# Attention products on four 64x64 TensorE tiles, in bursts inside pass 2

## The chip, the cores and the metric

One core of one Trainium2 chip runs the whole program. The metric is the device time of one execution in microseconds (us), as a median over executions. Engines: TensorE (PE, with PEld for its weight loads), VectorE (DVE), ScalarE (ACT), GpSimd (POOL), and SyncE (SP), which here only starts transfers.

## The reference, cut to what matters

```python
# q, k, v: [8 batches, 8 heads, 576 rows, 64]
q_s = softmax(q, axis=-1)            # over the 64
k_s = softmax(k, axis=2)             # over the 576 rows
kv  = einsum('bhsd,bhse->bhde', k_s, v)      # 64x64 per head
out = einsum('bhsd,bhde->bhse', q_s, kv)
x   = out as [4608 tokens, 512]
h   = x @ w_in                       # [512, 2048]
y   = (h * sigmoid(beta * h)) @ w_out        # [2048, 512], 4608x512 out
```

The two large products are most of the work. Attention is small, but its contraction (64) and its output (64) fill half of the 128*128 weights, which the trace shows for the large products, in each direction.

## The kernel before

The kernel cuts the 4608 tokens into nine slabs of 512: eight hold 512 rows of one batch each, and the ninth holds the 64 remaining rows of all eight. Pass 1 of a slab is 64 products with `w_in` and 16 Silus; pass 2 is 64 products with `w_out`. Products of a later batch's attention are put between them. Two heads share a product: the keys of the pair are laid out block-diagonally with zeros, so that one 128x128 weight holds both.

```python
# keys and values: 9 products for each pair of heads, 36 per batch, 65 columns each
# (the 65th column of v is 1 and gives the softmax denominator)
l, r_, ke, kv, ko = kv_rows(b, hp, j)        # l = EK[i][:, hp, j, 0:128], half zeros
mm(PS[bk][:, VW * n:VW * n + D + 1], l, r_[:, 0:D + 1], j == 0, j == NG - 1, ...)

# output: one product of 512 columns per pair, 4 per batch; KVD is block-diagonal too
mm(PS[bk][:, :], KVD[i][:, hp, :], QT[i][:, hp, :], True, True, ...)

def attn(b):                                 # b = slab + 1; numbers are places in the slab
    s = spread(kv_steps(b, (0, 1, 2, 3)), 8, 36)         # amid pass 1
    ...                                                  # four outputs in 84 to 108
    if b % 2: s += spread(outr_steps(b), 104, 120)       # remaining rows of two batches
```

A small recording layer orders the engines.

```python
def add(self, eng, fn, r=(), w=(), bank=(), ...):
    for k in w:                              # whoever read or wrote what this overwrites
        for d in self.readers.get(k, ()): deps.append(d)
    ...
def plan(self):
    for op in self.ops:
        for d in op.deps:
            d.inc = True                     # d is to raise its engine's semaphore
```

The softmax here doesn't subtract the row's maximum and nothing guards it: scores larger than these inputs give would overflow.

## Time and profile before

| | before |
|---|---|
| time, median | 284.99 us (284.67 to 285.23, 3 runs) |
| profiled span | 283.6 us |
| TensorE busy | 97% |

The page and the stretches of the kernel before are shown and priced in the prediction. A burst, below, is a run of products on tiles with no product of the whole array between them.

### The profile page before, as it was taken

How to read it: one execution, taken by the hardware profiler on the slowest of the kernel's cores; microseconds unless marked ns; L12 is line 12 of the kernel's file. 1: busy time of each engine (PE TensorE's matmuls, PEld its weight loads, DVE VectorE, ACT ScalarE, POOL GpSimd, SP SyncE). 2: the span in 40 equal slices, each digit the busy share in tenths (PEclk: the TensorE clock that was granted, in tenths of full speed). 3: DMA queues.
4: the chain of work that ended last, by engine and by line, in shares of the span. 5: the costliest groups of instructions: out<-in, count | busy, mean ns of one | idle time of the engine just before them, and what ended most of it. 6: DMA issues, size and time to landing. Idle time of an engine off the chain costs nothing.

```text
span 283.6 us, 3916 instructions
## 1 busy us (share of the span) xinstructions
PE 276.3 (97%) x1575; PEld 136.4 (48%) x1606; DVE 116.4 (41%) x217; ACT 177.2 (62%) x242; POOL 39.3 (14%) x58
## 2 busy tenths in 40 slices
PE   7899999999999999999999999999999999999995
PEld 3545454445455445544554445444544445444443
DVE  4655686208791348124741564055705300110012
ACT  5667777989977936796479737892660076017500
POOL 6632041216122032100130000000000000000000
PEclk9799999999999999999999999999999999999999
DMA  7999999999998999207970033002700030012022
GB/s 244 375 391 399 391 369 301 364 345 236 321 345 235 363 354 308 39 21 255 373 112 1 2 148 74 2 1 92 132 19 0 0 150 0 0 49 102 0 74 74
DMA packets 41466, 50.07 MB, mean 177 GB/s; under 512 B 20324, under 2 KB 28772, under 8 KB 40296
## 3 DMA queue, kind: packets, MB, share of 16 engines
q1 hardware_dynamic: 40496, 48.77, 55.4%
q10 hardware_dynamic: 952, 1.06, 1.1%
q8 instruction: 12, 0.20, 0.3%
q14 instruction: 6, 0.05, 0.0%
HBM read 36.71 MB, written 9.44 MB: 163 GB/s over the span
## 4 chain that ended last, share of the span: by engine, by line
PE 93%; DMA 3%; SPq 2%; issue 1%; POOL 1%; DVE 0%; POOLq 0%
PE PS L373 92%; DMA WST<-in_moe_w_in_dram 3%; SPq L259 1%; POOL WIN L580 1%; SPq L249 0%; PE PS L371 0%; SPq L576 0%; DVE O2S L732 0%; POOLq L140 0%
## 5 line engine op out<-in xcount | busy, mean ns | idle before, releaser
L654 ACT ACTIVATE GT<-PS,BETA 128x512 bf16<-128x512 f32 x144 | 96.7, 689 | 79.7 <-PE PS L373 79.6
L373 PE MATMUL PS<-WOUT,GT 128*128 128x512 bf16 (+2 forms) x580 | 131.8, 373 | 0.6
L373 PE MATMUL PS<-XT,WIN 128*128 128x512 bf16 x560 | 130.7, 379 | 0.5
L373 PEld LDWEIGHTS PS<-XT,WIN 128*128 128x128 bf16 x576 | 60.2, 106 | 58.9 <-ACT GT L654 0.4
L373 PEld LDWEIGHTS PS<-WOUT,GT 128*128 128x128 bf16 x592 | 55.4, 98 | 61.8
L711 DVE COPY O2S<-PS 128x512 f32<-128x512 f32 x33 | 22.7, 687 | 107.7 <-PE PS L373 107.7
L373 PE MATMUL PS<-VB,EK 128*128 128x65 bf16 x252 | 33.3, 193 | 0.4
L358 POOL CAST VB<-VF 128x576 bf16<-128x576 f32 x29 | 21.6, 746 | 77.9 <-DMA VF<-in_v_dram 48.8
L309 ACT ACTIVATE EK<-KF 64x1152 bf16<-64x1152 f32 x24 | 27.8, 1158 | 0.4
L339 DVE TENSOR_REDUCE QS<-EQ 128x8 f32<-128x512 bf16 (+1 forms) x22 | 20.1, 913 | 16.0 <-ACT EQ L297 15.8
L373 PEld LDWEIGHTS PS<-VB,EK 128*128 128x128 bf16 x252 | 20.0, 98 | 6.5
L449 DVE CAST XT<-PS 128x512 bf16<-128x512 f32 x24 | 16.4, 690 | 10.9 <-PE PS L373 10.9
L297 ACT ACTIVATE EQ<-QF 128x512 bf16<-128x512 f32 x32 | 17.8, 619 | 1.4 <-DMA QF<-in_q_dram 1.2
L341 DVE TENSOR_TENSOR EQ<-EQ,QI 128x1024 bf16<-128x1024 bf16 (+1 forms) x14 | 15.9, 1133 | 0.5
L373 PE MATMUL PS<-QT,KVD 128*128 128x512 bf16 x29 | 11.2, 387 | 0.2
L341 POOL TENSOR_TENSOR EQ<-EQ,QI 128x512 bf16<-128x512 bf16 x8 | 8.3, 1044 | 18.4 <-DVE QI L340 18.1
L411 DVE TENSOR_TENSOR KVD<-PS,RC 64x64 bf16<-64x64 f32 (+2 forms) x28 | 8.6, 308 | 0.9
L297 ACT ACT_TABLE_LOAD x6 | 7.7, 1283 | 0.1
L373 PE MATMUL PS<-XT 128*128 128x512 f32 x6 | 5.5, 1088 | 1.5 <-DVE XT L219 1.5
L654 ACT ACT_TABLE_LOAD x5 | 6.4, 1283 | 0.1
L373 PEld LDWEIGHTS PS<-QT,KVD 128*128 128x128 bf16 x32 | 3.1, 98 | 5.6 <-DVE KVD L411 1.2
L432 DVE RECIPROCAL RC<-PS 128x4 f32<-128x4 f32 (+2 forms) x9 | 1.6, 176 | 10.0 <-PE PS L373 9.9
(54 smaller groups left out, 90.0 us busy)
## 6 DMA issues: line engine op xcount, KB each, us to landing
out_dram<-O2S SPq DMA_DIRECT2D x8, 1024.0 KB, 5.0
KF<-in_k_dram SPq DMA_DIRECT2D x6, 1152.0 KB, 9.0
VF<-in_v_dram SPq DMA_DIRECT2D x6, 1152.0 KB, 11.3
QF<-in_q_dram SPq DMA_DIRECT2D x6, 1024.0 KB, 7.6
KF<-in_k_dram SPq DMA_DIRECT2D x8, 288.0 KB, 8.6
VF<-in_v_dram SPq DMA_DIRECT2D x8, 288.0 KB, 9.0
WST<-in_moe_w_in_dram SPq DMA_DIRECT2D x8, 256.0 KB, 8.1
O2S<-in_moe_w_in_dram SPq DMA_DIRECT2D x4, 512.0 KB, 11.4
```

The costliest lines, as they stand in the source:

```text
L259: add(engs[c % len(engs)], lambda e, a=a, o=o: e.dma_start(o, a), w=[(name, i, hp) for hp in range(c * n, c * n + n)], slot=f"{name}{i}_{c}")
L297: add(ACTE, lambda e, o=o, a=a: e.activation(o, a, ACT.Exp), r=[("qf", i, hp)], w=[("eq", i, hp)])
L309: add(ACTE, lambda e, o=o, a=a: e.activation(o, a, ACT.Exp), r=[("kf", i, h) for h in hps], w=[("ek", i, h, e_) for h in hps])
L339: add(DVE, lambda e: e.tensor_reduce(s_, a, AX.X, ALU.add), r=ks, w=[("qs", i, hp0)])
L341: add(eng, lambda e: e.tensor_tensor(a, a, vb, ALU.mult), r=ks + [("qi", i, hp0)], w=ks)
L358: add(eng, lambda e: (e.copy if eng == ACTE else e.tensor_copy)(o, a), r=[("vf", i, hp), ("vone", i)], w=[("vb", i, hp, h) for h in ((0, 1 ...
L373: add(PE, lambda e: e.matmul(o, l, r_, start=start, stop=stop, tile_position=tp), r=r, w=w, bank=[bk])
L411: add(DVE, lambda e, o=o, a=a, s_=s_: e.tensor_tensor(o, a, s_, ALU.mult), r=[("ps", bk)] + [("rc", i, h) for h in hps], w=[("kvd", i, h, ...
L449: add(eng, lambda e: (e.copy if eng == ACTE else e.tensor_copy)(XT[i][:, hp, :], PS[bk][:, :]), r=[("ps", bk)], w=[("xt", i, hp)], bank=[bk])
L580: add(eng, lambda e: e.tensor_copy(WIN[:, m, 512 * c:512 * c + 512], STAGE[c][:, m, :]), r=[SKEY[c][m]], w=[("win", c, m)])
L654: add(ACTE, lambda e: e.activation(GT[:, f, :], PS[bk][:, :], ACT.Silu, scale=BETA[:, f:f + 1]), r=[("ps", bk), "beta"], w=[("gt", f)], ba ...
L711: add(eng, lambda e: (e.copy if eng == ACTE else e.tensor_copy)(O2S[t % 2][:, u, :], PS[bk][:, :]), r=[("ps", bk)], w=[("o2", t % 2, u)], ...
```

## The change: its intent and its core

The intent is to stop multiplying zeros. The array is used as four independent 64x64 tiles: four products, a quad of two heads of one pair and two of the next, are to run at once. The kernel puts the tiles of an odd pair off the diagonal, so a head whose keys stand in partitions 0 to 63 has its result written to 64 to 127; therefore the queries of odd pairs are loaded with their two heads swapped. The keys need no zeros any more, so one exponential covers 128 partitions. The tile products stand in bursts, since going between the full array and tiles costs time (0.22 us in the one burst of the kernel before).

```diff
+        def quad(hp):     # (pair, first row, first column of the tile)
+            return ((hp, 0, 0), (hp, 64, 64), (hp + 1, 0, 64), (hp + 1, 64, 0))
+        def kv_quads(b, bks, halves=(0, 2)):
+            for a in halves:
+                for j in range(NG):
+                    for hp, ro, co in quad(a):
+                        tile_mm(bks[hp % 2], ro, co, VW * (a // 2), D + 1,
+                                EK[i][p, hp, j, :], VB[i][p, hp, j, 0:D + 1], ...)
+        def out_quads(b, bks): ...     # 8 products of 512 columns, 2 evictions on ACT, 2 on DVE
+        def outr_quads(b, bks): ...    # 16 products of 64 columns
-        def attn(b):
-            s = spread(kv_steps(b, (0, 1, 2, 3)), 8, 36)
...
-                todo = spread(outr_steps(1), 101.5, 103) + attn_late(2)
+                todo = spread(outr_steps(1), 94, 95)
+                todo += [(95, lambda: kv_a(2)), (103, lambda: kv_b(2)),
+                         (117, lambda: block(2, True)), (125, lambda: kv_b(3))]
+            elif t < 7 and t % 2 == 0:
+                todo = [(80, lambda: block(t + 1, False))]      # 8 outputs + 16 remainders
+                if t + 2 < B:
+                    todo += [(93, lambda: kv_a(t + 2)), (101, lambda: kv_b(t + 2))]   # 36 + 36
             elif t < 7:
-                todo = attn(t + 1)
+                todo = [(93, lambda: block(t + 1, True)), (101, lambda: kv_b(t + 2))] # 44 + 36
...
-            load_main("qf", qt_h, QF, b)
+            load_swapped(b)            # four transfers in place of one
```

More of the change, by code (lines that the diff above doesn't have):

```diff
@@ L181, in bass_efficient_attn_shen__then__act_swish_beta_kernel @@
         EQ = [sb(f"EQ{i}", [128, NHP, 4, 2, D], BF16) for i in range(2)]
-        EK = [sb(f"EK{i}", [128, NHP, NG, 2 * D], BF16) for i in range(2)]
+        EKD = sb("EKD", [128, NHP, NG, 2 * D], BF16)
+        EK = [sb(f"EK{i}", [128, NHP, NG, D], BF16) for i in range(2)]
         EQR = [sb(f"EQR{i}", [128, H, D], BF16) for i in range(2)]
@@ L191, in bass_efficient_attn_shen__then__act_swish_beta_kernel @@
         KVD = [sb(f"KVD{i}", [128, NHP, 128], BF16) for i in range(2)]
+        KVC = [sb(f"KVC{i}", [128, NHP, D], BF16) for i in range(2)]
         RC = [sb(f"RC{i}", [128, NHP], F32) for i in range(2)]
@@ L232, in homes_vk, with homes_ek @@
                 add(POOL, lambda e, z=z: e.memset(z.bitcast(F32), 0.0), w=[("kvz", i, e_)])
-        def homes_ek(i, e_, r=()):
-            z = EK[i][64 * e_:64 * e_ + 64, :, :, 64 * (1 - e_):64 * (2 - e_)]
-            add(POOL, lambda e: e.memset(z.bitcast(F32), 0.0), r=r, w=[("ekz", i, e_)])
+        def homes_ek(e_):
+            z = EKD[64 * e_:64 * e_ + 64, :, :, 64 * (1 - e_):64 * (2 - e_)]
+            add(POOL, lambda e: e.memset(z.bitcast(F32), 0.0), w=[("ekz", e_)])
         def src(th, b, h0, nh):
@@ L262, in load_qrem @@
         def load_qrem(b):
+            i = b // 2 % 2
             for h in range(2):
-                a = bass.AP(qt_h, (b + h) * H * S * D + SM * D, [[D, SR], [S * D, H], [1, D]])
-                i = b // 2 % 2
-                add(SP, lambda e, h=h, a=a: e.dma_start(QRF[i][64 * h:64 * h + 64, :, :], a),
-                    w=[("qrf", i, h)], slot=f"qrf{i}{h}")
+                q0 = (b + h) * H * S * D + SM * D
+                if b == 0:
+                    a = bass.AP(qt_h, q0, [[D, SR], [S * D, H], [1, D]])
+                    add(SP, lambda e, h=h, a=a: e.dma_start(QRF[i][64 * h:64 * h + 64, :, :], a),
+                        w=[("qrf", i, h)], slot=f"qrf{i}{h}")
+                    continue
+                for x, (s0, d0, n) in enumerate(SLOTS):
+                    a = bass.AP(qt_h, q0 + s0 * S * D, [[D, SR], [n * S * D, 2], [1, D]])
+                    o = bass.AP(QRF[i], 64 * h * H * D + d0 * D,
+                                [[H * D, 64], [n * D, 2], [1, D]])
+                    add(SP, lambda e, o=o, a=a: e.dma_start(o, a),
+                        w=[("qrf", i, h, x)], slot=f"qrf{i}{h}{x}")
         def load_k(b, split=1, cs=None, engs=(SP,)):
@@ L273, in load_v, with load_swapped @@
             load_pairs("vf", vt_h, VF, b, split, cs)
+        SLOTS = ((0, 0, 1), (4, 4, 1), (2, 3, 4), (3, 2, 4))
+        def load_swapped(b):
+            i = b % 2
+            for x, (s0, d0, n) in enumerate(SLOTS):
+                a = bass.AP(qt_h, (b * H + s0) * S * D,
+                            [[4 * D, 128], [n * S * D, 2], [1, 4 * D]])
+                o = bass.AP(QF[i], d0 * 4 * D, [[H * 4 * D, 128], [n * 4 * D, 2], [1, 4 * D]])
+                add(SP, lambda e, o=o, a=a: e.dma_start(o, a),
+                    w=[("qf", i, hp, x) for hp in ((0,), (2,), (1, 3), (1, 3))[x]],
+                    slot=f"qs{i}{x}")
         def load(b):
-            load_main("qf", qt_h, QF, b)
+            load_swapped(b)
             load_k(b)
@@ L297, in exp_q @@
                 add(ACTE, lambda e, o=o, a=a: e.activation(o, a, ACT.Exp),
-                    r=[("qf", i, hp)], w=[("eq", i, hp)])
-        def exp_k(b, hp0=0, n=4, step=1):
-            i = b % 2
-            for hp in range(hp0, hp0 + n, step):
-                hps = range(hp, hp + step)
-                for e_ in range(2):
-                    o = bass.AP(EK[i], 64 * e_ * NHP * NG * 128 + hp * NG * 128 + 64 * e_,
-                                [[NHP * NG * 128, 64], [128, NG * step], [1, 64]])
-                    a = bass.AP(KF[i], 64 * e_ * NHP * KW + hp * KW,
-                                [[NHP * KW, 64], [64, NG * step], [1, 64]])
-                    add(ACTE, lambda e, o=o, a=a: e.activation(o, a, ACT.Exp),
-                        r=[("kf", i, h) for h in hps], w=[("ek", i, h, e_) for h in hps])
+                    r=[("qf", i, hp)] if b < 2 else [("qf", i, hp, x) for x in
+                                                     ((2, 3) if hp % 2 else (hp // 2,))],
+                    w=[("eq", i, hp)])
         def exp_kh(b, hp, n, e_):
             i = b % 2
-            o = bass.AP(EK[i], 64 * e_ * NHP * NG * 128 + hp * NG * 128 + 64 * e_,
+            o = bass.AP(EKD, 64 * e_ * NHP * NG * 128 + hp * NG * 128 + 64 * e_,
                         [[NHP * NG * 128, 64], [128, NG * n], [1, 64]])
@@ L320, in exp_kh, with exp_kc @@
                 r=[("kf", i, h) for h in hps], w=[("ek", i, h, e_) for h in hps])
-        def exp_kc(hp):
-            o = bass.AP(GT, hp * KW, [[NF * SM, 128], [1, KW]])
-            a = bass.AP(KF[0], hp * KW, [[NHP * KW, 128], [1, KW]])
-            add(ACTE, lambda e: e.activation(o, a, ACT.Exp), r=[("kf", 0, hp)], w=[("ekc", hp)])
+        def exp_kc(b, hp, n=1):
+            i = b % 2
+            o = bass.AP(EK[i], hp * KW, [[NHP * KW, 128], [1, n * KW]])
+            a = bass.AP(KF[i], hp * KW, [[NHP * KW, 128], [1, n * KW]])
+            add(ACTE, lambda e: e.activation(o, a, ACT.Exp),
+                r=[("kf", i, h) for h in range(hp, hp + n)],
+                w=[("ekc", i, h) for h in range(hp, hp + n)])
         def exp_qr(pi):
@@ L329, in exp_qr @@
             add(ACTE, lambda e: e.activation(EQR[i][:, :, :], QRF[i][:, :, :], ACT.Exp),
-                r=[("qrf", i, 0), ("qrf", i, 1)], w=[("eqr", i)])
+                r=[("qrf", i, h) for h in range(2)] + [("qrf", i, h, x) for h in range(2)
+                                                       for x in range(4)], w=[("eqr", i)])
         def norm_main(b, hp0, n, eng=DVE):
@@ L398, in kv_rows @@
             i = b % 2
-            return (EK[i][:, hp, j, :], VB[i][:, hp, j, :],
-                    [("ek", i, hp, 0), ("ek", i, hp, 1), ("ekz", i, 0), ("ekz", i, 1)],
+            return (EKD[:, hp, j, :], VB[i][:, hp, j, :],
+                    [("ek", i, hp, 0), ("ek", i, hp, 1), ("ekz", 0), ("ekz", 1)],
                     [("vb", i, hp, 0), ("vb", i, hp, 1)], [("vone", i)])
@@ L483, in outr_steps, with tile_mm @@
             return [lambda hp=hp, e_=e_: one(hp, e_) for hp in range(NHP) for e_ in range(2)]
-        def attn(b):
-            s = spread(kv_steps(b, (0, 1, 2, 3)), 8, 36)
-            x = []
-            for hp in range(NHP):
-                x += out_step(b, hp)
-            s += spread(x, 84, 108)
-            if b % 2:
-                s += spread(outr_steps(b), 104, 120)
-            return s
-        def attn_late(b):
-            s = spread(kv_steps(b, (0, 1)), 103, 105.5) + spread(kv_steps(b, (2, 3)), 106, 110)
-            x = []
-            for hp in range(NHP):
-                x += out_step(b, hp, MB)
-            return s + spread(x, 112, 124)
+        def tile_mm(bk, ro, co, c, w, l, r_, start, stop, r):
+            mm(PS[bk][co:co + 64, c:c + w], l, r_, start, stop, r=r, w=[("ps", bk)], bk=bk,
+               tp=(ro, co))
@@ new lines, in quad @@
+        def quad(hp):
+            return ((hp, 0, 0), (hp, 64, 64), (hp + 1, 0, 64), (hp + 1, 64, 0))
+        def kv_quads(b, bks, halves=(0, 2)):
+            i = b % 2
+            for a in halves:
+                for j in range(NG):
+                    for hp, ro, co in quad(a):
+                        p = slice(ro, ro + 64)
+                        tile_mm(bks[hp % 2], ro, co, VW * (a // 2), D + 1, EK[i][p, hp, j, :],
+                                VB[i][p, hp, j, 0:D + 1], j == 0, j == NG - 1,
+                                [("ekc", i, hp), ("vb", i, hp, 0), ("vb", i, hp, 1), ("vone", i)])
+            for y in range(2 if 2 in halves else 0):
+                bk = bks[y]
+                s_ = bass.AP(PS[bk], D, [[512, 128], [VW, 2]])
+                v_ = bass.AP(RC[i], y, [[NHP, 128], [2, 2]])
+                vb = bass.AP(RC[i], y, [[NHP, 128], [2, 2], [0, D]])
+                p_ = bass.AP(PS[bk], 0, [[512, 128], [VW, 2], [1, D]])
+                o = bass.AP(KVC[i], y * D, [[NHP * D, 128], [2 * D, 2], [1, D]])
+                add(DVE, lambda e, v_=v_, s_=s_: e.reciprocal(v_, s_), r=[("ps", bk)],
+                    w=[("rc", i, y), ("rc", i, y + 2)], bank=[bk])
+                add(DVE, lambda e, o=o, p_=p_, vb=vb: e.tensor_tensor(o, p_, vb, ALU.mult),
+                    r=[("ps", bk), ("rc", i, y), ("rc", i, y + 2)],
+                    w=[("kvc", i, y), ("kvc", i, y + 2)], bank=[bk])
@@ new lines, in out_quads @@
+        def out_quads(b, bks):
+            i = b % 2
+            for a in (0, 2):
+                for hp, ro, co in quad(a):
+                    p = slice(ro, ro + 64)
+                    tile_mm(bks[hp], ro, co, 0, SM, KVC[i][p, hp, :], QT[i][p, hp, :], True, True,
+                            [("kvc", i, hp), ("qt", i, hp)])
+            for hp in range(NHP):
+                eng, bk = (ACTE if hp % 2 else DVE), bks[hp]
+                add(eng, lambda e, eng=eng, bk=bk, hp=hp: (
+                    e.copy if eng == ACTE else e.tensor_copy)(XT[i][:, hp, :], PS[bk][:, :]),
+                    r=[("ps", bk)], w=[("xt", i, hp)], bank=[bk])
@@ new lines, in outr_quads @@
+        def outr_quads(b, bks):
+            pi = b // 2
+            for a in (0, 2):
+                for e_ in range(2):
+                    for hp, ro, co in quad(a):
+                        p = slice(ro, ro + 64)
+                        tile_mm(bks[hp % 2], ro, co, 256 + (a // 2) * 128 + e_ * 64, 64,
+                                KVC[e_][p, hp, :], QTR[p, hp, 64 * e_:64 * e_ + 64], True, True,
+                                [("kvc", e_, hp), "qtr"])
+            for y in range(2):
+                o = bass.AP(XT8, y * SM + pi * 128, [[NM * SM, 128], [2 * SM, 2], [1, 128]])
+                p_ = bass.AP(PS[bks[y]], 256, [[512, 128], [128, 2], [1, 128]])
+                add(DVE, lambda e, o=o, p_=p_: e.tensor_copy(o, p_), r=[("ps", bks[y])],
+                    w=[("xt8", pi, y), "xw"], bank=[bks[y]])
@@ L502, in spread, with kv_a, kv_b, block @@
+        def kv_a(b):
+            kv_quads(b, (1, 2), (0,))
+        def kv_b(b):
+            kv_quads(b, (1, 2), (2,))
+        def block(b, kv):
+            out_quads(b, (5, 6, 7, 0))
+            if kv:
+                kv_a(b + 1)
+            else:
+                outr_quads(b, (1, 2))
         def spread(steps, lo, hi):
@@ L532, in kv_tiles @@
                     p = slice(64 * e_, 64 * e_ + 64)
-                    mm(PS[bk][p, 0:D + 1],
-                       bass.AP(GT, 64 * e_ * NF * SM + hp * KW + j * D, [[NF * SM, 64], [1, D]]),
+                    mm(PS[bk][p, 0:D + 1], EK[0][p, hp, j, :],
                        VB[0][p, hp, j, 0:D + 1], j == 0, j == NG - 1,
-                       r=[("ekc", hp), ("vb", 0, hp, 0), ("vb", 0, hp, 1), ("vone", 0)],
+                       r=[("ekc", 0, hp), ("vb", 0, hp, 0), ("vb", 0, hp, 1), ("vone", 0)],
                        w=[("ps", bk)], bk=bk, tp=(64 * e_, 64 * e_))
@@ L604, in bass_efficient_attn_shen__then__act_swish_beta_kernel @@
         homes_vk(0)
-        homes_ek(0, 0)
-        homes_ek(0, 1)
+        homes_ek(0)
+        homes_ek(1)
         homes_vk(1)
@@ L613, in bass_efficient_attn_shen__then__act_swish_beta_kernel @@
         for hp in range(NHP):
-            exp_kc(hp)
+            exp_kc(0, hp)
             if hp < 2:
@@ L647, in pass1_mm @@
             x = XT8 if t == 8 else XT[t % 2]
-            rd = [("xt8", p_) for p_ in range(4)] if t == 8 else [("xt", t % 2, m)]
+            rd = [("xt8", 0)] + [("xt8", p_, y) for p_ in range(1, 4) for y in range(2)] if t == 8 else [("xt", t % 2, m)]
             n = 2 if f < 8 else 4
@@ L693, in bass_efficient_attn_shen__then__act_swish_beta_kernel @@
                 at(m)
-        for e_ in range(2):
-            homes_ek(1, e_, [("win", 3, NM - 1)])
         load_wout(0)
@@ L846, in bass_efficient_attn_shen__then__act_swish_beta_kernel @@
                 nb = [2, 3]
+            late = []
             for b in nb:
-                exp_q(b)
-                if b == 2:
+                if t == 1 and b == 2:
+                    exp_q(2)
                     for hp in range(2):
@@ L852, in bass_efficient_attn_shen__then__act_swish_beta_kernel @@
                     t_dma(2, 0, 2)
-                if b % 2 == 1:
-                    exp_qr(b // 2)
-                exp_k(b, step=2)
+                for hp in (0, 2):
+                    exp_kc(b, hp, 2)
+                if b > 2:
+                    late.append(b)
                 if b > 3:
@@ L858, in bass_efficient_attn_shen__then__act_swish_beta_kernel @@
                         cast_v(b, hp)
+            for b in late:
+                exp_q(b)
+                if b % 2 == 1:
+                    exp_qr(b // 2)
                 if b + 2 < B and t > 1:
```

## The prediction

Passages that no trace or run of this case shows are cut from the text below, and the cuts are marked. That four tiles share one slot was not shown by any run then: the kernel before has only pairs, 2 to 4 ns apart. The nine slots of 0.030 us for 36 products, the four of 0.03 for 16 remainders, and the two of 0.216 for eight products of 512 columns, are the estimate from a pair's slot and a full product's time. The size of the second rival's tail is a guess that no trace supports. That an exponential on 128 partitions takes what one on 64 takes is in the trace of before: 684 ns on 128x576 (L325), 682 on 64x576 (L319).

> **What bounds the kernel now.** I read the busy table and the 40 slices first, then the chain that ended last, then stretches of the two passes, then TensorE's timeline at the attention products.
>
> ```profile
> PE 276.3 (97%) x1575; PEld 136.4 (48%) x1606; DVE 116.4 (41%) x217; ACT 177.2 (62%) x242; POOL 39.3 (14%) x58
> ...
> PE   7899999999999999999999999999999999999995
> ...
> PEclk9799999999999999999999999999999999999999
> ...
> PE 93%; DMA 3%; SPq 2%; issue 1%; POOL 1%; DVE 0%; POOLq 0%
> ...
> L654 ACT ACTIVATE GT<-PS,BETA 128x512 bf16<-128x512 f32 x144 | 96.7, 689 | 79.7 <-PE PS L373 79.6
> L373 PE MATMUL PS<-WOUT,GT 128*128 128x512 bf16 (+2 forms) x580 | 131.8, 373 | 0.6
> ```
>
> The reader is to see that TensorE is never idle after the first slices, at full clock; 93% of the chain that sets the end is its products, and ScalarE waits 79.6 us for it. So this is a question of counting TensorE's stream: what shortens it counts, what frees ScalarE or VectorE does not. A product's own record (373 ns) is longer than its share of the stream, since products overlap; I price by spacing. The kernel goes through nine slabs of tokens, each pass 1 (64 products XT,WIN) and pass 2 (64 products WOUT,GT), with attention of a later batch mixed in. Stretches from pass start to pass start give its price (columns: stretch, its length, then busy time and count of each engine):
>
> ```profile
> 60.34:76.39 16.05, 15.88 (x110) 8.02 (x112) 10.60 (x23) 15.66 (x20) 5.81 (x7) 1.00 1.05 289
> ...
> 106.24:121.17 14.93, 14.82 (x99) 7.77 (x100) 7.02 (x10) 10.29 (x15) 3.30 (x4) 1.00 0.60 168
> 121.17:135.84 14.68, 14.62 (x68) 6.66 (x68) 4.75 (x7) 10.52 (x13) 0.00 (x0) 1.00 0.50 165
> 225.14:238.96 13.81, 13.76 (x64) 6.75 (x64) 0.69 (x1) 10.29 (x15) 0.00 (x0) 1.00 0.19 77
> ```
>
> The last is a bare pass: 13.81 / 64 = 0.216 us per product of 512 columns. The second holds one batch's 36 key-value products (block-diagonal keys, 128x128 weights, 65 columns): 14.93 - 13.81 = **1.12 us**, 0.031 each. The third holds its four output products of 512 columns: 14.68 - 13.81 = **0.87 us**. The first holds both for batch 2, and eight 64-column products for the remaining rows of a batch pair: 2.24 - 1.12 - 0.87 = **0.25 us**; another pass 2, from 91.33 to 106.24, has out and remainder in 14.91, which gives 0.23.
>
> At full clock the trace also has one burst on tiles, of batch 0 (two diagonal 64x64 tiles, 18 products in nine pairs):
>
> ```profile
> 14.44 0.38 PE L373 MATMUL PS<-QT,KVD 128*128 128x512 bf16 x1
> 14.75 0.47 PE L373 MATMUL PS<-VB,GT 64*64 64x65 bf16 x18
> 15.15 0.82 PE L373 MATMUL PS<-XT,WIN 128*128 128x512 bf16 x3
> ```
>
> From the first product to the first on tiles is 0.31 us instead of 0.216: **0.09 to enter**. From there to the next full product is 0.40. In the start times of single products the two of a pair are 2 to 4 ns apart and the pairs mostly 29 to 35 ns. Nine slots at 0.030 are 0.27, which leaves **0.13 to leave**, first slot's filling included. So 0.22 us per burst is fixed.
>
> [...]
>
> **The change part by part.**
> - Removed: attention of batches 2 to 7 on the whole array. Six batches of keys and values 6 x 1.12 = 6.7; six of outputs 6 x 0.87 = 5.2; three remainders 3 x 0.23 = 0.7. Sum **12.6 us, all of it on the path**. Half of the array multiplied zeros in these.
> - Added on tiles: half a batch of keys and values is 36 products of 64x64, in nine slots of four. 12 halves x 9 x 0.030 = 3.2. Outputs: eight products of 512 columns in two slots, 12 x 0.216 = 2.6. Remainders: 16 products of 64 columns in four slots, 12 x 0.03 = 0.4. Sum **6.2 us**.
> - Added for switching: the built order of TensorE has 15 bursts: in slab 1 36, 36, 44, 36; in slabs 2 and 4 24, 36, 36; in slabs 3 and 5 44, 36; in slab 6 24. 15 x 0.22 = **3.3 us**. Before, these products needed no switch.
> - Moved: keys and values of batch b go from pass 1 of slab b-1 to the end of pass 2 of slab b-2. Their exponentials now come first on ScalarE after the Silus, in 12 instructions of 128 partitions in place of 24 of 64 partitions (24 x 1.158 = 27.8 us; an estimate by half, 13.9, as the free size is the same). Two of four output evictions per batch go to ScalarE (12 x about 0.58, from the like eviction's mean of 582 ns). VectorE loses those. None is on the path.
> - Loads: the odd head pairs are swapped by splitting a query load into four and a remainder load into four. The bytes stay; SyncE issues three more per batch and six more per pair of remainder loads, at 0.4 to 0.7 us each as its queue now takes, beside a queue with long gaps.
> - Two memsets of 1.05 us on GpSimd go; nothing on the path waited for them.
>
> Net: 12.6 - 6.2 - 3.3 = 3.1 us saved. From 285.0 that gives **281.9 us**, 1.1% less. The first slab, its start and the last two slabs are unchanged.
>
> **Where an input could come late.** Slab 1 is tightest: ScalarE must do the exponentials of batches 2 and 3. Pass 2 starts at 60.34; the first key burst stands 31 products in, at about 67.3. Batch 2's queries end at 64.7 in before's timeline, so its first keys come at about 65.9 and all at 67.1: a margin of a microsecond or more. Batch 3's values were cast by 71.8, and its burst stands at about 73. Elsewhere the first key burst is 29 products (6.3 us) into pass 2, and table load and both key exponentials take 1.3 + 2 x 1.16 = 3.6 after the last Silu. Transposed queries are issued by about 87 in slab 2 and land 4.2 later at worst, before about 93.7, when the burst stands. I expect no wait.
>
> **Rivals.**
> - *Four tiles run only two abreast*[...]. For: the trace has diagonal pairs alone.[...] Keys and values would then cost 6.5, total saving -0.2: 285.2. If outputs went by two as well, 5.2 for 2.6: 287.8.
> - *The instruction stream becomes the bound*: a burst of 36 is 72 instructions in 0.27 us, one per 4 ns[...]. For: nothing in before ran so densely for so long. Against: before, eighteen products with their loads went at one product per 16 ns or so, and a pair's members 2 to 4 ns apart. A tail of 0.1 to 0.25 us per burst, a guess at the size, takes 1.5 to 3.7 us: 283.4 to 285.6.
> - *Switching is dearer or cheaper*: it rests on one burst. At 0.15 per burst the time is 280.8, at 0.35 it is 283.9.
> - *A new wait* for keys, transposes or the two evictions on ScalarE: 1 us in a slab at most a few times, 283 to 285.
> - *ScalarE's relief pays*: it waits 79.6 us for TensorE already, so 0.
>
> **Range and chances.** All errors that I can name but cheaper switching lengthen the time, so the range leans up: 280.4 to 285.2. Over 2% faster means under 279.3, that is 5.7 of the 6.4 us which tiles at no switching cost would give: 0.03. Over 2% slower means above 290.7, more than two-abreast tiles everywhere: 0.03. Within 2%: 0.94.
>
> **What would show it.** Right: bare pass 1 stretches of 13.81 us in slabs 2 to 6 (before 14.93); pass 2 of an even slab longer by about 0.43 + 0.12 + 0.54 + 3 x 0.22 = 1.75, of an odd slab by 0.43 + 0.54 + 2 x 0.22 = 1.4; a burst of 36 taking about 0.4 us from its first product to the next full one; the key exponential at about 1.16 us on 128 partitions, x12. Wrong: tile products with starts 15 ns apart instead of 8 (two abreast, or instruction-bound[...]); gaps before a burst with a releaser named; TensorE idle over 1 us in sum after the start.

## The result, and the profile after

The changed kernel took **283.73 us** (283.52 to 283.89, 4 runs) against 285.0 us; the ratio is 0.9956, 95% interval 0.9938 to 0.9973. In a second, larger set of the same kernel it was 283.94 against 285.14 us, ratio 0.9952 (0.9937 to 0.9966). A ratio here is the mean time of one kernel's fast runs over that of the other's fast runs of the same rounds, so it is not quite the ratio of the medians. So the change gains 0.4 to 0.5%, some 1.3 us, where 3.1 us were forecast. The time lies within the stated range; the gain is well under half of the forecast.

The page after, in the lines that answer to those of before:

```profile
PE 273.1 (97%) x1835; PEld 133.2 (47%) x1870; DVE 106.2 (38%) x211; ACT 168.6 (60%) x242; POOL 36.1 (13%) x56
...
PE   7899999999999999999999999999999999999995
...
PEclk9799999999999999999999999999999999999999
...
L723 ACT ACTIVATE GT<-PS,BETA 128x512 bf16<-128x512 f32 x144 | 96.8, 689 | 81.8 <-PE PS L390 81.8
L390 PE MATMUL PS<-WOUT,GT 128*128 128x512 bf16 (+2 forms) x569 | 126.8, 373 | 1.7 <-issue 0.5
```

TensorE is the bound as before, at the same clock. ScalarE is freed by 8.6 us of work (177.2 to 168.6), and that shortens nothing: its wait for TensorE is 81.8 us, after 79.7. So the answer must lie in TensorE's stream. The stretches from pass start to pass start of the changed kernel (slab 1 pass 2, then both passes of slab 2 and both of slab 3; first columns are the stretch and its length):

```profile
60.18:77.36 17.19, 16.73 (x221) 8.51 (x224) 8.83 (x19) 13.46 (x19) 5.79 (x7) 1.00 1.06 275
77.36:91.18 13.81, 13.71 (x63) 6.75 (x64) 8.62 (x14) 10.28 (x15) 3.01 (x4) 1.00 1.10 293
91.18:106.96 15.79, 15.52 (x158) 7.35 (x160) 4.76 (x11) 8.53 (x12) 2.67 (x4) 1.00 1.05 325
106.96:120.78 13.81, 13.76 (x64) 6.74 (x64) 5.90 (x7) 10.28 (x15) 2.67 (x4) 1.00 0.99 224
120.78:136.31 15.54, 15.27 (x142) 7.33 (x144) 4.19 (x9) 9.04 (x13) 0.00 (x0) 1.00 0.58 182
```

Pass 1 is bare, 13.81 us, as predicted: the 12.6 us were removed. But pass 2 of slab 2 is longer than a bare one by 15.79 - 13.81 = 1.98 us where 1.75 was forecast, that of slab 3 by 1.73 for 1.4, and that of slab 1 by 3.38 for 2.6 (the same prices, with 0.23 for the remainders of batches 0 and 1, which stay on the whole array). Over all six slabs the tiles cost 11.0 us in this trace, where 9.5 were priced. The time went into the bursts. TensorE's timeline at two bursts of 36 in slab 2, then two in slab 4 of the same kernel:

```profile
98.32 0.56 PE L390 MATMUL PS<-VB,EK 64*64 64x65 bf16 x36
98.81 1.90 PE L390 MATMUL PS<-WOUT,GT 128*128 128x512 bf16 x7
100.64 0.56 PE L390 MATMUL PS<-VB,EK 64*64 64x65 bf16 x36
101.13 0.61 PE L390 MATMUL PS<-WOUT,GT 128*128 128x512 bf16 x2
```

```profile
157.27 0.48 PE L390 MATMUL PS<-VB,EK 64*64 64x65 bf16 x36
157.91 1.67 PE L390 MATMUL PS<-WOUT,GT 128*128 128x512 bf16 x7 [0.16 <-issue]
159.51 0.48 PE L390 MATMUL PS<-VB,EK 64*64 64x65 bf16 x36
159.93 0.82 PE L390 MATMUL PS<-WOUT,GT 128*128 128x512 bf16 x3
```

The same 36 products take 0.49 us to the next full product in slab 2 (98.32 to 98.81) and 0.42 in slab 4 (159.51 to 159.93). (At 157.91 a record is missing: the first full product stands some 0.22 earlier.) In the start times of single products, the four of a quad are mostly 3 to 4 ns apart and the quads mostly 29 to 35 ns, in all slabs: the four tiles do run abreast. The two tiles of a pair, on rows 0 and 64, write one bank on different partitions at that distance, with correct results. But in slabs 1 to 3 the last three products of 36, and the last seven of 44, follow one another at 33 to 35 ns instead of some 8. That is a tail that looks like the second rival of the prediction. Every burst of 36 and 44 in slabs 1 to 3 has it, none in slabs 4 and 5. The bursts of 44 in slab 1, then in slab 5 (eight outputs, then 36 keys):

```profile
73.13 0.86 PE L390 MATMUL PS<-QT,KVC 64*64 64x512 bf16 x8
73.82 0.64 PE L390 MATMUL PS<-VB,EK 64*64 64x65 bf16 x36
...
185.93 0.63 PE L390 MATMUL PS<-QT,KVC 64*64 64x512 bf16 x8
186.39 0.51 PE L390 MATMUL PS<-VB,EK 64*64 64x65 bf16 x36
```

A ledger of the bursts, each from the start of the full product ahead of it to the start of the one after, less the 0.216 us that a full product takes anyway:

| bursts | priced, us each | measured, us each | sum over price |
|---|---|---|---|
| six of 36, slabs 1 to 3 | 0.49 | 0.58 | 0.54 |
| three of 36, slabs 4, 5 | 0.49 | 0.51 | 0.06 |
| 44 in slab 1 | 0.92 | 1.35 | 0.43 |
| 44 in slab 3 | 0.92 | 1.12 | 0.20 |
| 44 in slab 5 | 0.92 | 0.99 | 0.07 |
| three of 24 | 0.77 | 0.78 | 0.01 |

(Where the record of the full product after a burst is missing, one more product's time is taken off.) The overrun is 1.3 us. By the stretches it is 1.5: the full product after a burst is also followed some 10 ns late, which the ledger leaves out, 0.15 us in 15 bursts. Two things stand out: the tail, and an extra in slab 1, where the second quad of output products starts 0.21 us later than elsewhere.

### The profile page after: what moved, and what is told of

It reads as the page before. It is cut to its first block, busy times and chain, and to the rows that moved or that the text cites. A ratio compares the mean times of both kernels' runs of the same rounds, so it can differ in the third digit from the quotient of the medians.

```text
span 281.8 us, 4474 instructions
## 1 busy us (share of the span) xinstructions
PE 273.1 (97%) x1835; PEld 133.2 (47%) x1870; DVE 106.2 (38%) x211; ACT 168.6 (60%) x242; POOL 36.1 (13%) x56
## 4 chain that ended last, share of the span: by engine, by line
PE 89%; ACT 4%; issue 2%; DVE 2%; DMA 1%; POOL 0%; ACTq 0%; POOLq 0%
PE PS L390 88%; ACT EQ L320 2%; DMA QF<-in_q_dram 1%; ACT L339 1%; PE PS L388 1%; ACT EK L339 1%; DVE QS L356 0%; POOL EQ L358 0%; ACT EQR L345 0%; ACT XT L540 0%; DVE KVD L428 0%; DVE EQ L358 0%; DVE KVC L527 0%; DVE RC L525 0%; DVE QI L357 0%
## 5 line engine op out<-in xcount | busy, mean ns | idle before, releaser
L723 ACT ACTIVATE GT<-PS,BETA 128x512 bf16<-128x512 f32 x144 | 96.8, 689 | 81.8 <-PE PS L390 81.8
L390 PE MATMUL PS<-WOUT,GT 128*128 128x512 bf16 (+2 forms) x569 | 126.8, 373 | 1.7 <-issue 0.5
L390 PE MATMUL PS<-XT,WIN 128*128 128x512 bf16 x565 | 125.8, 379 | 0.6
L540 DVE CAST XT<-PS 128x512 bf16<-128x512 f32 x12 | 7.7, 686 | 33.8 <-PE PS L390 33.8
L339 ACT ACTIVATE EK<-KF 128x1152 bf16<-128x1152 f32 (+1 forms) x16 | 15.9, 1035 | 1.7 <-DMA KF<-in_k_dram 1.5
L390 PEld LDWEIGHTS PS<-VB,EK 64*64 64x64 bf16 x504 | 7.3, 109 | 5.2 <-issue 3.9
L540 ACT CAST XT<-PS 128x512 bf16<-128x512 f32 x12 | 6.3, 577 | 4.8 <-PE PS L390 4.8
L390 PE MATMUL PS<-VB,EK 64*64 64x65 bf16 x504 | 8.8, 195 | 0.0
L332 ACT ACTIVATE EKD<-KF 64x576 bf16<-64x576 f32 (+1 forms) x6 | 5.0, 841 | 1.0 <-DMA KF<-in_k_dram 0.9
L525 DVE RECIPROCAL RC<-PS 128x2 f32<-128x2 f32 x12 | 2.0, 165 | 8.8 <-PE PS L390 8.8
L357 DVE RECIPROCAL QI<-QS 128x8 f32<-128x8 f32 (+1 forms) x22 | 5.0, 226 | 0.8
```

The source lines that it names most:

```text
L332: add(ACTE, lambda e: e.activation(o, a, ACT.Exp), r=[("kf", i, h) for h in hps], w=[("ek", i, h, e_) for h in hps])
L339: add(ACTE, lambda e: e.activation(o, a, ACT.Exp), r=[("kf", i, h) for h in range(hp, hp + n)], w=[("ekc", i, h) for h in range(hp, hp + n)])
L357: add(DVE, lambda e: e.reciprocal(v_, s_), r=[("qs", i, hp0)], w=[("qi", i, hp0)])
L390: add(PE, lambda e: e.matmul(o, l, r_, start=start, stop=stop, tile_position=tp), r=r, w=w, bank=[bk])
L540: add(eng, lambda e, eng=eng, bk=bk, hp=hp: (e.copy if eng == ACTE else e.tensor_copy)(XT[i][:, hp, :], PS[bk][:, :]), r=[("ps", bk)], w=[ ...
L723: add(ACTE, lambda e: e.activation(GT[:, f, :], PS[bk][:, :], ACT.Silu, scale=BETA[:, f:f + 1]), r=[("ps", bk), "beta"], w=[("gt", f)], ba ...
```

## The experiments

Theories after the result. **A**: instruction supply; a burst of 72 instructions outruns it, and transfers, busy in slabs 1 to 3 and idle in slabs 4 and 5, slow it. **B**: the place in the instruction stream. **C**, formed later: semaphore raises. Beside these stands the question which part of the change earns its gain.

### The changed kernel again

> The changed kernel again, as the measure for the runs beside it: a ratio of about 0.9955 to before. The trace of the first run shows 12 bursts of keys and values: in slabs 1 to 3 the last three products of a burst of 36, and the last seven of a burst of 44, follow one another at 34 to 35 ns instead of 8. If that is a property of this kernel's place and not an accident of one run, this trace shows it in the same bursts and in none of slabs 4 and 5.

Measured: median of six runs 283.94 us, ratio 0.9952. The profiled execution, alone of all, ran at a granted clock of 0.757 and took 360.94 us, so its times are not compared; the other five executions were fast. Its start times do answer the question asked: every burst of 36 and 44 in slabs 1 to 3 ends in single products 28 to 35 ns apart, and none in slabs 4 and 5 does.

### Outputs alone on tiles

```diff
-            if kv: kv_a(b + 1)
-            else:  outr_quads(b, (1, 2))
+            if not kv: outr_quads(b, (1, 2))
...
```

Keys and values go back to the whole array, 36 products amid pass 1 of the slab before (batch 2's in pass 2 of slab 1). The keys with their zeros return, for odd pairs anti-diagonal, so that the result lies as the tiles leave it. To make room for them the edit also moves some small buffers into the space of others.

> Only outputs and remainders go on tiles (6 bursts in place of 15); keys and values are multiplied on the whole array amid pass 1, as before the change. Theory (the switch costs 0.22 us per burst, and half a batch of keys and values on tiles costs 0.51 to 0.58 us with it, against 0.56 on the whole array): the key part gains nothing, so this run keeps the whole gain: six outputs 0.87 to 0.65, three remainders 0.23 to 0.13, 1.6 us below before, 283.4 us. Rival (keys on tiles carry a good part of the gain): it loses that, 284.2 us or more.

Measured: 285.3 us, ratio 1.0005 (0.9993 to 1.0017): no gain at all. The trace says why, and it is this kernel's own fault. Slab 1's pass 2 took 17.49 us; in the run after this one, which mends it, it took 16.04. ScalarE's timeline there:

```profile
64.50 9.45 ACT L348 ACTIVATE EKX<-KF 64x1152 bf16<-64x1152 f32 x8
73.97 2.19 ACT L319 ACTIVATE EQ<-QF 128x512 bf16<-128x512 f32 x4
76.06 0.61 ACT L377 ACTIVATE EQR<-QRF 128x512 bf16<-128x512 f32 x1
76.58 1.05 ACT L570 CAST XT<-PS 128x512 bf16<-128x512 f32 x2
```

The exponentials of 64 partitions are back, 9.45 us in one slab, and two of the output evictions that slab 2 needs stand behind them. With these two on VectorE the run was made again:

```diff
-                eng, bk = (ACTE if hp % 2 else DVE), bks[hp]
+                eng, bk = (ACTE if hp % 2 and b > 2 else DVE), bks[hp]
```

> The kernel with outputs alone on tiles again, with batch 2's four output evictions all on VectorE: in the first such run ScalarE made them after 9.5 us of key exponentials and slab 2 began 1.4 us late, which was that kernel's fault. The bursts themselves cost 0.65 and 0.78 us as worked out. Theory: the 1.4 us come back, 283.8 us, as fast as the changed kernel, so that keys on tiles are worth nothing in it. Rival: 284.5 us or more.

Measured: **283.83 us**, ratio 0.9955 (0.9943 to 0.9967), the same as the full change. Its burst of eight outputs:

```profile
126.08 1.03 PE L422 MATMUL PS<-WOUT,GT 128*128 128x512 bf16 x4
127.04 0.63 PE L422 MATMUL PS<-QT,KVC 64*64 64x512 bf16 x8
127.60 0.60 PE L422 MATMUL PS<-WOUT,GT 128*128 128x512 bf16 x2
```

From 127.04 to 127.60 are 0.56 us, and 0.09 to enter: 0.65 instead of 0.87 us. So outputs and remainders on tiles, six bursts, earn as much as the full change, and in the changed kernel the keys and values on tiles, nine bursts more, earn nothing that the times can tell. The bursts agree: by the ledger the keys cost 6.5 us on tiles (in a burst of 44 what is over 0.65, in slab 1 with its extra), where 6.7 were removed.

### Both key halves in one burst

```diff
-    (93, lambda: kv_a(t + 2)), (101, lambda: kv_b(t + 2))       # 36 + 36
+    (101, lambda: kv_ab(t + 2))                                 # 72; likewise 80 for 44 + 36
```

> Both halves of a batch's keys and values in one burst of 72 (80 with the outputs): 9 bursts in place of 15. Theory of switching cost alone: 6 x 0.22 = 1.3 us less than the changed kernel, 282.4 us, all bursts at 8 ns per product. Theory of a bound instruction stream (some 66 instructions at full rate, then one product per 34 ns in slabs 1 to 3, none such in slabs 4 and 5): 39 or more products at 26 ns too much are 1.0 us in each of four bursts, so 285 to 286 us, slower than the changed kernel, with the loss in slabs 1 to 3 and a gain of 0.2 us in each of slabs 4 and 5.

Measured: 285.3 us, ratio 1.0009 (0.9996 to 1.0022). Slower than the changed kernel of the same rounds by 1.4 us, though six switches are gone. The burst of 72 in slab 2 and that in slab 4:

```profile
100.81 1.79 PE L390 MATMUL PS<-VB,EK 64*64 64x65 bf16 x72
102.53 1.04 PE L390 MATMUL PS<-WOUT,GT 128*128 128x512 bf16 x4
...
161.04 0.83 PE L390 MATMUL PS<-VB,EK 64*64 64x65 bf16 x72
161.81 0.82 PE L390 MATMUL PS<-WOUT,GT 128*128 128x512 bf16 x3
```

They take 1.72 and 0.77 us to the next full product. In slab 2 all but the first 33 or so products of the burst come at 34 ns; in slab 4 none does. So length alone is not the limit: 72 products with their 72 weight loads ran at full rate in slab 4, in 0.64 us from first to last start, 9 ns per product. The number came out as theory A said, and A was still wrong, as the next run shows.

### No transfers at the bursts

```diff
         def load(b):
+            if b > 3:
+                return          # wrong result on purpose: batches 4 to 7 reuse old data
```

> Wrong result on purpose: the loads of batches 4 to 7 are left out, so the DMA engines are idle at the bursts of slabs 2 and 3 and nearly so late in slab 1; TensorE's stream is the same. Theory (the slow tail comes from instruction supply that DMA traffic slows): no tail at 34 ns in slabs 2 and 3, bursts of 36 take 0.29 us from first to last start instead of 0.37, about 0.5 to 0.7 us less in all, 283.1 us. Rival (the tail belongs to the place in the instruction stream): tails unchanged, 283.7 us.

Measured: 283.61 us, ratio 0.9951, as the changed kernel. Two stretches of three us, at the bursts of slab 2 and of slab 4 (the last two columns are the transfers' share and GB/s), then the bursts of slab 2:

```profile
98.00:101.00 3.00, 3.00 (x80) 1.48 (x79) 0.69 (x1) 1.94 (x3) 1.11 (x2) 1.00 0.02 5
157.00:160.00 3.00, 3.00 (x83) 1.49 (x82) 0.69 (x1) 1.89 (x3) 0.00 (x0) 1.00 0.00 0
```

```profile
98.35 0.56 PE L392 MATMUL PS<-VB,EK 64*64 64x65 bf16 x36
98.84 1.90 PE L392 MATMUL PS<-WOUT,GT 128*128 128x512 bf16 x8
```

The transfers are gone (share 0.02 in the first stretch, against 1.13 in the changed kernel), and the tail is exactly the same. Theory A falls in its form with the transfers.

### One raise per wait

What else differs between slabs 3 and 4? Counting in the program which TensorE products raise the semaphore gave it: in slabs 1 to 3 all 36 of 36 and 44 of 44, in slabs 4 and 5 none to four per burst of 36 or 44. The recording layer marks every product that read a buffer as soon as a later batch overwrites that buffer. Batches 6 and 7 have no successor. This is theory C. The edit keeps only the last of the products that an instruction must wait for:

```diff
         for op in self.ops:
+            last = max((d.pos for d in op.deps if d.eng == PE), default=-1)
+            op.deps = [d for d in op.deps if d.eng != PE or d.pos == last]
             for d in op.deps:
                 d.inc = True
```

The edit is sound only if products end in program order. That was the assumption, and no trace here shows it, since the ends of products are modelled; the four kernels here that carry the edit gave correct results.

> The changed kernel with one edit in its bookkeeping: of several TensorE products that an instruction of another engine must wait for, only the last one raises the semaphore[...]. In the changed kernel's program every product of the bursts in slabs 1 to 3 raises it (36 of 36, 44 of 44), because a later batch overwrites the buffers that it reads; in slabs 4 and 5 it is 0 to 4 of them. Theory (the slow tail is the raising of semaphores, about 34 ns each once some 33 products have gone by): all bursts of 36 take 0.29 us from first to last start, 44 about 0.30 for their key part, total 0.506 per burst of 36 with its switch; about 0.8 us less than the changed kernel, 283.1 us. Rival (instruction supply by place in the stream): tails remain, 283.9 us.

Measured: **282.89 us**, ratio 0.9918 (0.9904 to 0.9932), 1.0 us less than the changed kernel, by their ratios to the kernel before, as the rounds differ. In slab 2 the bursts now look like slab 4's:

```profile
98.10 0.48 PE L392 MATMUL PS<-VB,EK 64*64 64x65 bf16 x36
98.52 1.90 PE L392 MATMUL PS<-WOUT,GT 128*128 128x512 bf16 x7
100.35 0.48 PE L392 MATMUL PS<-VB,EK 64*64 64x65 bf16 x36
100.76 0.60 PE L392 MATMUL PS<-WOUT,GT 128*128 128x512 bf16 x2
```

0.41 to 0.42 us to the next full product in place of 0.49. B falls as well: the products stand at the same places. The profiled execution was the slowest of its seven (284.32 us). TensorE waited in slab 1 for the transposed queries of batch 2:

```profile
73.12 0.86 PE L392 MATMUL PS<-QT,KVC 64*64 64x512 bf16 x8 [0.88 <-DMA QT<-EQ]
```

It now reaches that burst sooner than they land. This is also the extra of slab 1 in the ledger: in the changed kernel their second half lands 0.4 us after the burst's start, and the second quad of outputs starts 0.21 us late.

How the raises make the tail is in the same trace files, which also hold the times at which the semaphore was raised (the views do not print them). Within a burst the raises land one by one, some 34 ns apart, so they fall behind products that start every 8 ns. In slab 2 of the changed kernel, at the burst of 98.32, three of them land 0.297, 0.331 and 0.365 us after its first start, and the last three products start at 0.301, 0.335 and 0.370. Counted at every start, products begun and not yet raised, the one that starts included, reach 31 and never more: in all 32 bursts with a tail of the changed kernel, of the merged one, of the run without transfers and of the converse below, each slow product starts with exactly 31. That is the 34th product of a burst of 36, when three raises have landed, and the 38th of a burst of 44, when seven have. With one raise per wait at most 4 wait.

### The converse, and a control

```diff
+        for op in self.raising:      # every product on tiles
+            op.inc = True            # raises that nothing waits for
```

> The converse: the changed kernel in which every product on tiles raises the semaphore, in slabs 4 and 5 too, where 8 of 152 key and output products did. Nothing waits for the added raises. Theory of semaphores: the bursts of slabs 4 and 5 get the tail too (36 products from 0.29 to 0.37 us, the key part of 44 from 0.30 to 0.45), 3 x 0.08 + 0.15 = 0.4 us more than the changed kernel, 284.3 us; bursts of 24 stay at 0.78. Rival (something else sets slabs 1 to 3 apart): slabs 4 and 5 unchanged.

Measured: 283.93 us, ratio 0.9964 (0.995 to 0.9978), which the time alone cannot tell from the changed kernel's 0.9952. The trace can; slab 4 has the tail now:

```profile
159.51 0.56 PE L393 MATMUL PS<-VB,EK 64*64 64x65 bf16 x36
160.00 0.60 PE L393 MATMUL PS<-WOUT,GT 128*128 128x512 bf16 x2
```

0.49 us instead of 0.42. In slab 5 the key part of the burst of 44 went from 0.30 to 0.45 us from first to last start, as expected. Raises alone, with nothing else moved, make the tail; that is shown in both directions. The size is clean from the start of slab 2 to the end, where the start of the kernel and slab 1's wait play no part. The changed kernel, this one, and the one with one raise per wait:

```profile
77.36:281.80 204.44, 199.49 (x1264) 96.31 (x1287) 63.92 (x105) 110.33 (x156) 11.88 (x16) 1.00 0.42 118
77.29:282.05 204.76, 199.84 (x1264) 96.67 (x1287) 63.42 (x105) 110.33 (x156) 14.30 (x16) 1.00 0.40 118
77.15:281.24 204.09, 199.13 (x1264) 95.91 (x1287) 62.67 (x103) 110.32 (x156) 12.01 (x16) 1.00 0.43 120
```

Raises added in slabs 4 and 5 cost 0.32 us; raises taken out of slabs 2 and 3 save 0.35. Three bursts of 36 and one of 44 are 3 x 0.076 + 0.13 = 0.36 by the ledger. The same single-raise edit on the kernel before:

> The control: the kernel before with the same edit (only the last product waited for raises the semaphore). There no two small products follow one another for long, so the raises are hidden: ratio to before 0.999 to 1.001. Rival (raises cost every product something): below 0.998, and the gain of the edited kernels would not be the bursts' alone.

Measured: 284.75 us, ratio 0.9996 (0.9981 to 1.0012). The kernel before raised as often, but with 0.216 us products in between it cost nothing that can be seen: from the start of slab 2 to the end both traces take 207.19 us.

### The switch by itself

```diff
+            elif t == 7:             # kernel before; 16 bursts of four small products
+                todo = [(67 + 3.5 * n, empty) for n in range(16)]
```

> The switch by itself: the kernel before with 16 bursts of four products of 64x64 weights and 64 columns (zeros, written to banks that nothing reads) put into pass 2 of slab 7, which holds no attention. Theory: each costs 0.09 to enter and 0.12 to leave and at most 0.02 of work, 0.22 us; 16 x 0.22 = 3.5 us, 288.6 us. Rival (entering and leaving overlap with the neighbours when the burst is short): under 0.1 each, 286 us.

Measured: 289.26 us, ratio 1.0148 (1.0132 to 1.0165). Pass 1 of slab 7, then pass 2 with the 16 bursts:

```profile
224.86:238.68 13.81, 13.76 (x64) 6.76 (x64) 0.69 (x1) 10.29 (x15) 0.00 (x0) 1.00 0.19 77
238.68:256.64 17.96, 17.59 (x126) 6.75 (x128) 2.08 (x3) 0.71 (x2) 0.00 (x0) 1.00 0.00 1
```

(17.96 - 13.81) / 16 = **0.26 us** for a burst with next to no work in it: 0.093 to enter, as priced, about 0.15 to leave, and 0.01 each for the four starts and for the late product after it. The 0.22 that was expected here is too little.

### Fewer bursts, with one raise per wait

The merged kernel with the single-raise edit, and then all tile products of a slab in one burst of up to 96 (7 bursts; the evictions follow the whole burst):

```diff
-    (80, block(t + 1, False)), (93, kv_a(t + 2)), (101, kv_b(t + 2))
+    (95, one_burst(t + 1, t + 2, True))       # 8 outputs, 72 keys, 16 remainders
```

> The merged kernel (9 bursts, 72 or 80 products where both halves are) with the same edit. Theory of semaphores: all bursts of 72 run like those of slab 4 in the run without the edit, 0.86 us with the switch instead of 1.81; sum of bursts 9.2 us against 10.9 in the changed kernel, 282.2 us. Rival (instruction supply): as before, 285.3 us.

> With one raise per wait, all tile products of a slab in one burst (outputs, both key halves of the next batch, remainders): 7 bursts in place of 15, of 24 to 96 products. Theory of switching cost plus semaphores: sum of bursts about 8.6 us against 10.9 in the changed kernel, 281.6 us. Rival (a limit on a burst's length[...]): products beyond the first 33 slow down, 284 us or more.

Measured: 282.05 us, ratio 0.9891 (0.9877 to 0.9905), and **280.87 us**, ratio 0.9852 (0.9838 to 0.9867). The burst of 96 in slab 2:

```profile
96.66 0.63 PE L392 MATMUL PS<-QT,KVC 64*64 64x512 bf16 x8
97.11 0.86 PE L392 MATMUL PS<-VB,EK 64*64 64x65 bf16 x72
97.79 0.32 PE L392 MATMUL PS<-QTR,KVC 64*64 64x64 bf16 x16
```

The 72 key products take 0.68 us (97.11 to 97.79) and no tail shows. So the rival, a limit on length, falls. The same six switches that made the merged kernel 1.4 us slower with the raises make it 0.8 us faster without: 282.05 against 282.89. This last kernel beats both, 4.4 us below the kernel before and 3.1 below the changed one, by medians of different rounds for the latter.

Not all of that is the bursts'. From the start of slab 2 to the end the changed kernel takes 204.44 us, one raise per wait 204.09, merged as well 203.43, in one burst 203.08; the kernel before takes 207.19. So 1.4 us of the step from the changed kernel to this last one lie there. Most of the rest lies in the first slab, which ended at 44.32 us in this trace and at 45.42 in the changed kernel's. All four profiled runs with the single-raise edit, and the merged one, left it earlier (44.3 to 45.0) than the other seven fast ones (45.3 to 45.6); why is open. That 1.1 us is more than the 0.7 us by which the last run came out below its expected 281.6.

## Why the prediction was right or wrong, point by point

**The bound** was right: TensorE at full clock, and what freed ScalarE, VectorE and GpSimd bought nothing.

**Removed, 12.6 us**: right. All pass 1 stretches of slabs 2 to 6 are 13.81 us after the change.

**Four tiles abreast**: right. A clean burst of 36 costs 0.51 us with its switch against 0.49 priced; the key exponentials were 1152 ns each, x12, as worked out; the first rival (two abreast) falls.

**Added on tiles, 3.2 us for the keys**: this is the step that failed. It priced nine slots at 0.030 and took for granted that a product costs its slot. In slabs 1 to 3 every product also raised a semaphore, and once 31 raises were waiting, the raises set a pace of 34 ns. By the difference of like bursts that is 6 x 0.076 = 0.46 in the bursts of 36, and 0.13 (1.12 - 0.99) in each of two bursts of 44: 0.7 us in the traces, confirmed in slabs 2 and 3, 4 and 5 by 0.35 and 0.32. Removing the raises gave 1.0 us in the timed runs, with an interval wide enough for 0.7; what else may be in it is the earlier start named above. The second rival foresaw a tail of the right form, but put it down to the instruction stream and kept it out of the central number. The runs showed that 72 products in a row, and 96 in a mixed burst, run without a tail when no more than 10 of them raise.

**Switching, 3.3 us**: a second, smaller miss. It rested on one burst, at 0.22. A clean burst of 36 less its 0.27 of slots leaves 0.24, an empty burst 0.26: 0.3 to 0.6 us too little over 15 bursts.

**No late input**: wrong by 0.2 us, in slab 1, for the second half of batch 2's transposed queries. For slab 1 margins were worked out for keys and values alone. The 4.2 us "at worst" for transposed queries is a misreading: in the trace of before it is the median from issue to landing, the longest is 6.9; in the changed kernel's slab 1 the first half took 6.8.

The three terms, 0.7, 0.3 to 0.6 and 0.2, make up the overrun of 1.3 to 1.5 us. The trace's saving of 1.6 us (12.6 - 11.0) and the timed 1.2 to 1.3 differ by less than the start varies from trace to trace (44.3 to 45.6 us at the first slab's end).

**What was missed in the sum**: it gave keys and values 6.7 removed, 3.2 added and 2.6 for the twelve bursts that hold them, so a gain near 0.9 us, and never asked whether that part was worth its nine extra switches. It was worth nothing that the times can tell: the run with outputs alone has the ratio 0.9955 against 0.9952.

Open: why 31 raises were waiting at most; why the first slab ends earlier in some kernels; why one execution of the changed kernel ran at a granted clock of 0.757 (360.94 us); and what makes the queries of slab 1 late. The split loads alone don't: the second run with outputs alone on tiles has them too, and there the second half landed at 72.24 us, a microsecond before its burst, where in the changed kernel it landed at 73.53.

## What to carry to other kernels

Before small products are packed into a dense burst, count which of them raise a semaphore. In these runs raises cost nothing that could be seen between 0.216 us products (in the kernel before 207.19 us from slab 2 to the end, with all of them and with one per wait), but set the pace, 34 ns each, where products came every 8 ns and 31 raises waited; raising at the last product alone was enough (282.89 us, and no tail). Price a change of tiling by the number of switches, 0.24 to 0.26 us each here, and put the tile work between as few switches as its inputs allow (280.87 us with 7 bursts). When an experiment gives the number that a theory foretold, still take the suspected cause away: here the transfers fitted every burst and had no part in it.
